# Threshold attention and a squared-relu MLP on one core: the sign of the weight rounding moves to ScalarE, and the first steps are started differently

## The chip, the cores and the metric

The kernel runs on one core of one Trainium2 chip. The metric is the device time of one execution in microseconds; before the change it is 1410.58 us (median of three runs, 1410.53 to 1411.54). The profile comes from one execution of the same program, which took 1409.49 us; its recorded instructions span 1407.7 us. The engines are named as the profile names them: PE is TensorE, PEld its weight loads, DVE is VectorE, ACT is ScalarE, POOL is GpSimd, SP is SyncE. A name with a q (SPq) is the engine's queue, where it issues transfers.

## The reference

An attention over 8 batches of 8 heads, 576 positions and 64 values a head, in which a score counts only if it lies within tau of its row's maximum; then a two-layer MLP on the 4608 rows of 512 values.

```python
scores = scale * np.matmul(q, k.transpose(0, 1, 3, 2))          # scale 1/8
thresh = np.max(scores, axis=-1, keepdims=True) - tau
scores = np.where(scores >= thresh, scores, -1000000000.0)
scores = scores - np.max(scores, axis=-1, keepdims=True)
attn = np.exp(scores)
attn = attn / (np.sum(attn, axis=-1, keepdims=True) + 1e-09)
x = np.matmul(attn, v)                                          # heads side by side: 4608 x 512
h = x @ w_in                                                    # w_in 512 x 2048
r = np.maximum(h, 0.0)
out = (r * r) @ w_out                                           # w_out 2048 x 512
```

The weights come in as 64-bit words of double-precision numbers, seen as pairs of 32-bit halves, and the kernel rounds them to fp32 itself.

## The kernel before, in words

**Visits and steps.** Two heads of a batch make a pair, and pairs are taken in visits. A visit's step handles 128 query rows of both heads; the 64 rows that are left over get a step of their own. For the first batch each pair is visited twice: the first two row blocks of all four pairs, then their rest, so that the first 256 tokens of the MLP are complete early. `steps` lists (visit, row block); the first two steps belong to visit 0, the third to visit 1.

**One step.** `scores(s)` multiplies q and k into two PSUM tiles of two banks each, `s0` and `s1` (L251), one for each head, and VectorE takes each row's maximum (L273). `exponents` lets ScalarE compute the bias and the threshold (L281, L282) and the exponential (L284). `threshold` compares the scores with the threshold, multiplies and sums (L296), and takes a reciprocal (L298, L299). `divide` scales on GpSimd (L304, L306). Two steps later `turn` transposes the result on TensorE against the identity into banks 4 to 7 (L330), ScalarE copies it to `wT` (L331), and `mix` multiplies with v (L432). The tiles `s0` and `s1` have one buffer each: L296 is their last reader, so the next step's scores wait for it. q and k are brought into matmul layout on VectorE (L230, `prep`); at a visit's last step the q and k of the next visit are prepared between `exponents` and `threshold`.

**The MLP** works in chunks of 256 tokens. `fill` takes its pieces from a queue and puts them between the attention's stages by a planner that spreads them over the remaining steps; L480 is the first layer, L490 and L491 relu and square, L516 the second layer of the first chunk, L549 that of the others, done with seven products in place of eight from sums of weights (L504) and of activations.

**Rounding the weights.** 32 pieces of 128 x 512 words are loaded into three areas in turn (`load_weights`, L125) and rounded in five stages (`round_weights`), spread over steps before the first MLP pieces need them. `words` is the raw data; `hi` and `lo` are every second 32-bit word of it. Stage 0, on ScalarE: `e` is the high half, read as an fp32 number and scaled by 2 to the -112 (L137), and `d` the low half, scaled (L138). Stage 1, on VectorE: the sign bit of `hi` is masked out (L140); `e` shifted left by 3 is combined with it (L141), which gives the upper part `t`. Stage 2: sign and exponent of `t` are masked out (L144). Stages 3 and 4, on GpSimd: `d` times that (L146), and added to `t` into the weights' place (L148). In most steps stage 1 stands on VectorE between the maxima and the thresholds; at a visit's last step, and for the second piece of a step that has two, it stands behind the thresholds.

**Order.** All five engines are scheduled by hand: each runs its instructions in the order in which the program lists them. Loads of q, k and v are issued by SyncE (`load_qk`, L173 and L175, `load_v`, L213), for the first visit by SyncE and ScalarE in turn, and later by GpSimd (L194). The two k loads of L175 in a visit are small: the last 64 rows of the odd head. The program has eight semaphores for the transfers of these two hardware queues, which are taken in turn. The identity, tau (L57, L58) and some constants (L79, L240) are set up at the head of the program.

Of the kernel before, what the change touches and what calls it, by code (L numbers as in the profile page):

```python
# [19 lines left out]
def kernel(  # L20
# [31 lines left out]
    psum = ctx.enter_context(tc.tile_pool(name="psum", bufs=1, space=bass.MemoryType.PSUM))  # L52

    ident = const.tile([P, P], FP32, name="ident")
    make_identity(nc, ident)
    ntau8 = const.tile([P, 1], FP32, name="ntau8")
    nc.gpsimd.dma_start(out=ntau8, in_=tau.to_broadcast([P, 1]))  # L57
    nc.vector.tensor_scalar(out=ntau8, in0=ntau8, scalar1=-1.0 / SCALE, scalar2=None, op0=ALU.mult)  # L58

    w_in_sb = const.tile([P, NMC, d_ff], FP32, name="w_in_sb")  # L60

# [14 lines left out]

    vs = [const.tile([P, 2 * NBLK + 2, D], FP32, name=f"vs{i}") for i in range(2)]
    qmid = const.tile([P, P], FP32, name="qmid")
    nc.gpsimd.memset(qmid, 0.0)  # L79
    at = RAW * 2 * WP  # L80
    w_slots = [const.tile([P, 2, S], FP32, name=f"w{i}") for i in range(2)]
    w_slots.append(spare[:, at:at + 2 * S].rearrange("p (u k) -> p u k", u=2))
# [16 lines left out]
    p5s = const.tile([P, HD], FP32, name="p5s")  # L99
    u_sum = const.tile([P, HD], FP32, name="u_sum")  # L100
    osb = const.tile([P, 2, d_model], FP32, name="osb")
    bank = {i: psum.tile([P, 512], FP32, tag=f"bank{i}", name=f"bank{i}") for i in range(4, 8)}


    n_in = d_ff // WP * NMC
# [14 lines left out]
    def weight_area(i):  # L120
        at = (i % RAW) * 2 * WP
        return spare[:, at:at + 2 * WP]
# [4 lines left out]
    def round_weights(i, stage):  # L127

        words = weight_area(i).bitcast(U32).rearrange("p (n w) -> p n w", w=2)
        lo, hi = words[:, :, 0], words[:, :, 1]
        t, e, d = (turned[:, (i % 3 * 3 + x) * WP:(i % 3 * 3 + x + 1) * WP] for x in range(3))
        tu, eu = t.bitcast(U32), e.bitcast(U32)
        if stage == 0:
            nc.scalar.activation(out=e, in_=hi.bitcast(FP32), func=AF.Copy, scale=2.0 ** -112)  # L137
            nc.scalar.activation(out=d, in_=lo, func=AF.Copy, scale=2.0 ** -52)  # L138
        elif stage == 1:
            nc.vector.tensor_scalar(out=tu, in0=hi, scalar1=0x80000000, scalar2=None, op0=ALU.bitwise_and)  # L140
            nc.vector.scalar_tensor_tensor(out=tu, in0=eu, scalar=3, in1=tu, op0=ALU.logical_shift_left,  # L141
                                           op1=ALU.bitwise_or)
        elif stage == 2:
            nc.vector.tensor_scalar(out=eu, in0=tu, scalar1=0xFF800000, scalar2=None, op0=ALU.bitwise_and)  # L144
        elif stage == 3:
            nc.gpsimd.tensor_tensor(out=d, in0=d, in1=e, op=ALU.mult)  # L146
        else:
            nc.gpsimd.tensor_tensor(out=weight_piece(i)[1], in0=t.rearrange("p (h d) -> p h d", h=2),  # L148
                                    in1=d.rearrange("p (h d) -> p h d", h=2), op=ALU.add)
# [11 lines left out]
    def load_qk(n):  # L161


        if by_dma(n):
            load_part(k, n)
            load_part(q, n)
            return
        for x, t in ((rows_of(n)[1], k), (rows_of(n)[0], q)):
            for m in range(4):
                src, to = rows_32(t, n, m), x[m * 32:(m + 1) * 32, :, :]  # L170
                queue = nc.scalar if n == 0 and m % 2 else nc.sync
                last = REST // 32 if t is k and m >= 2 else 0
                queue.dma_start(out=to[:, last:, :], in_=src[:, 0:S // 32 - last, :])  # L173
                if last:
                    queue.dma_start(out=to[:, 0:last, :], in_=src[:, S // 32 - last:, :])  # L175

    def load_part(t, n):
# [58 lines left out]
    LITTLE = 2.0 ** -20  # L236

    stats = [const.tile([P, 8, 2], FP32, name=f"st{i}") for i in range(4)]
    for st in stats:
        nc.gpsimd.memset(st[:, 4, :], S * LITTLE)  # L240
    weights = {}

    def scores(s):


        vis, i = steps[s]
        n = 2 if i < NBLK or paired(vis) else 1
        sc = [psum.tile([P, 2, 512], FP32, tag=f"s{u}", name=f"s{u}") for u in range(n)]

        def term(u, half, rows, lhsT, keys, to=slice(0, P)):  # L250
            nc.tensor.matmul(sc[u][to, half, 0:HALF], lhsT, keys[rows, half * HALF:(half + 1) * HALF],  # L251
                             start=True, stop=True)

        if i == NBLK and paired(vis):
            for half in range(2):
                for v_ in range(2):
                    for u in range(2):
                        rows, cols = slice(u * D, (u + 1) * D), slice(v_ * D, (v_ + 1) * D)
                        term(u, half, rows, qmid[rows, cols], kT[v_], cols)
        elif i == NBLK:  # L260
            for half in range(2):
                term(0, half, slice(0, P), qmid, kT[vis % 2])
        else:
            halves = [(half, u) for half in range(2) for u in range(n)]
            if early():
                halves.sort(key=lambda x: x[1])
            for half, u in halves:
                rows = slice(u * D, (u + 1) * D)
                term(u, half, rows, qT[rows, i * P:(i + 1) * P], kT[vis % 2])
        st = stats[s % len(stats)]  # L270
        mx = st[:, 0, 0:n]
        for u in range(n):
            nc.vector.tensor_reduce(out=mx[:, u:u + 1], in_=sc[u][:, :, 0:HALF], axis=AX.XY, op=ALU.max)  # L273

        w = w_slots[(s - first_dma) % (2 if by_dma(vis) else 3)][:, 0:n, :]
        weights[vis, i] = w, sc, st

    def exponents(vis, i):
        w, sc, st = weights[vis, i]
# [457 lines left out]
            prep_at[d].append(lambda n=nxt: prep_part(k, n + 1))  # L737

    load_qk(0)
    load_qk(1)  # L740
    load_v(0)
    for i in range(RAW):
        load_weights(i)
    prep(0)
    done = 0
    rounded_by = [0]
    for s in range(END + 1):
        state["step"] = s
        state["usable"] = rounded_by[-1]
        rounded_by.append(state["rounded"])  # L750
        on = s < NST
        now = []
        if on:
            n, i = steps[s]
            at = visits[n][1].index(i)
            last = at == len(visits[n][1]) - 1
            now = list(range(done, done + pieces[s]))
            done += pieces[s]
            more = n + 1 < len(visits)
            short = n < 2 * HP  # L760
            if short and at == 0 and 0 < n + 1 < 2 * HP:
                load_qk(n + 2)
            elif not short and at == 1 and not by_dma(n):
                load_qk(n + 1)
            if now:
                round_weights(now[0], 0)
            scores(s)
        old = steps[s - 2] if 2 <= s < NST + 2 and not by_dma(steps[s - 2][0]) else None
        at_once = now or old or early()
        lay = on and last and more and not by_dma(n)  # L770
        if old:
            turn(*old, 0)
            turn(*old, 1)
        if on:
            exponents(n, i)
            for p in now[1:]:
                round_weights(p, 0)
            if at == 1:
                split_left(n)
            if lay:  # L780
                prep(n + 1)
            elif now:
                round_weights(now[0], 1)
        if s in mixes and not old:
            mix(*mixes[s])
            for j in chunk_at.get(s, ()):
                add_chunk(j)
        quarter = rate(s) / 4 if s < END else 1e9
        fill(quarter)
        if s in mixes and old:  # L790
            mix(*mixes[s])
            for j in chunk_at.get(s, ()):
                add_chunk(j)
        if old:
            turn(*old, 2)
        state["free"] = s > first_dma
        if on:
            threshold(n, i)
            for fn in prep_at[s] + load_at[s]:
                fn()  # L800
            if lay and now:
                round_weights(now[0], 1)
            if now:
                round_weights(now[0], 2)
                round_weights(now[0], 3)
            for p in now[1:]:
                for stage in range(1, 4):
                    round_weights(p, stage)
            if not at_once:
                divide(n, i)  # L810
        if 0 < s <= NST and by_dma(steps[s - 1][0]):
            m, x = steps[s - 1]
            turn_blocks(m, x)
        for what in place_at[s]:
            place_blocks(*what)
        some_loads()
        fill(quarter)
        some_loads()
        if on and at_once:
            divide(n, i)  # L820
        fill(quarter)
        some_loads()
        fill(quarter)
        some_loads()
        if on:
            for p in now:
                end_rounding(p)
            if at == 0 and 0 < n <= 2 * HP:
                load_v(n)
            elif last and n >= 2 * HP and not by_dma(n):  # L830
                load_v(n + 1)
# [35 lines left out]
```

## Time and profile before

| what | us |
|---|---|
| time, median of three | 1410.58 |
| span of the profile | 1407.7 |
| MLP first layer, L480, TensorE busy | 522.3 |
| scores, L251, TensorE busy | 175.7 |
| rounding on VectorE, L140, L141, L144, busy | 18.0, 30.3, 17.6 |
| rounding on ScalarE, L137, L138, busy | 21.9, 21.5 |
| rounding on GpSimd, L146 and twice L148, busy | 41.0, 21.3, 21.3 |
| first rounding instruction starts | 19.5 |
| last one ends | 233.0 |

A busy time is a sum over all instructions of a row. Engines work beside each other, so such sums are not parts of the span: what an edit is worth depends on what else waits at that place. The column "idle before" of a row says how long its engine stood still ahead of those instructions, and "<-" what released it. The clock column gives the share of full speed that TensorE was granted by the records; before the first recorded change, at about 28 us, it shows 1.00 whatever the clock was.

### The profile page before, as it was taken

The page shows a single profiled execution, that of the slowest core. Times are in us where ns is not written, and L with a number is a line of the kernel's source. Part 1 is how long each engine was busy: PE and PEld are TensorE (multiplying, and loading weights), DVE is VectorE, ACT ScalarE, POOL GpSimd, SP SyncE. Part 2 cuts the span into 40 slices and gives each one's busy share as a digit, 9 for nine tenths or more (in the row PEclk, how much of TensorE's full clock was granted, in tenths as well). Part 3 has the DMA queues.
Part 4 walks back from the last instruction along what each step waited for, and adds up shares of the span by engine and source line. Part 5 has one row for each costly group of instructions (what it writes and reads, how often), then busy time and mean ns, then how long its engine had stood idle before and what let it go on. Part 6 is the DMA issues. An engine that isn't in the chain of part 4 may idle for free.

```text
span 1407.7 us, 22706 instructions
## 1 busy us (share of the span) xinstructions
PE 1359.6 (97%) x7556; PEld 1041.7 (74%) x7556; DVE 855.8 (61%) x1898; ACT 440.0 (31%) x1068; POOL 917.3 (65%) x1231
## 2 busy tenths in 40 slices
PE   5898998999999999999999999999999999999998
PEld 3676655767777777777777877777777877788887
DVE  5888785886767676766575666666666666501001
ACT  3775664323232323222222222222222222210110
POOL 3688778667787767777777858585867665422332
PEclk9998999999999999999999999999999999999999
DMA  7664441236555555554535455544545544310000
GB/s 150 135 143 124 117 104 42 59 71 122 107 115 98 118 99 111 101 104 85 107 82 111 99 111 96 101 82 102 93 98 95 123 83 97 64 38 15 1 16 16
DMA packets 397989, 127.95 MB, mean 91 GB/s; under 512 B 380464, under 2 KB 386672, under 8 KB 397872
## 3 DMA queue, kind: packets, MB, share of 16 engines
q1 hardware_dynamic: 374576, 93.07, 35.0%
q0 software_dynamic: 20912, 33.13, 8.6%
q8 instruction: 61, 1.00, 0.3%
q10 hardware_dynamic: 2384, 0.30, 0.1%
q14 instruction: 56, 0.46, 0.1%
HBM read 50.59 MB, written 9.44 MB: 43 GB/s over the span
## 4 chain that ended last, share of the span: by engine, by line
PE 88%; DVE 5%; ACT 2%; issue 2%; POOL 2%; DMA 1%; POOLq 0%; DVEq 0%; ACTq 0%
PE bank L480 34%; PE bank L549 28%; PE s L251 12%; PE bank L432 10%; PE bank L516 2%; PE bank L330 1%; DVE st L273 1%; DVE w L296 1%; DVE wo L504 1%; ACT w L284 1%; ACT wT L331 1%; DVE turned L141 1%; POOL kl L194 0%; DMA ql<-in_q_dram 0%; POOL w L306 0%
## 5 line engine op out<-in xcount | busy, mean ns | idle before, releaser
L480 PE MATMUL bank<-xT,w_in_sb 128*128 128x256 f32 x2304 | 522.3, 384 | 1.1 <-ACT osb L522 1.1
L480 PEld LDWEIGHTS bank<-xT,w_in_sb 128*128 128x128 f32 x2304 | 433.2, 191 | 83.3 <-issue 22.2
L273 DVE TENSOR_REDUCE st<-s 128x1 f32<-128x576 f32 x288 | 205.9, 752 | 231.2 <-PE s L251 231.1
L296 DVE SCALAR_TENSOR_TENSOR w<-s,st,w 128x576 f32<-128x576 f32 x269 | 209.2, 815 | 110.1 <-ACT w L284 109.9
L549 PE MATMUL bank<-wo,gsum 128*128 128x256 f32 x1088 | 248.9, 382 | 2.2 <-POOL gsum L470 2.1
L306 POOL TENSOR_SCALAR w<-w,st 128x576 f32<-128x576 f32 x269 | 223.3, 838 | 25.5 <-DVE st L299 19.3
L549 PEld LDWEIGHTS bank<-wo,gsum 128*128 128x128 f32 x1088 | 203.9, 190 | 41.3 <-issue 9.8
L491 POOL TENSOR_TENSOR g<-g 128x512 f32<-128x512 f32 x144 | 151.7, 1054 | 97.1 <-ACT g L490 95.6
L281 ACT ACTIVATE st<-st 128x2 f32<-128x2 f32 (+1 forms) x148 | 30.3, 205 | 576.5 <-DVE st L273 576.0
L251 PE MATMUL s<-kT,qT 64*128 64x288 f32 x1024 | 175.7, 440 | 32.2 <-DVE w L296 13.9
L549 PE MATMUL bank<-wo,g 128*128 128x256 f32 x816 | 188.3, 382 | 0.0
L284 ACT ACTIVATE w<-s,st 128x576 f32<-128x576 f32 x269 | 183.1, 731 | 0.2 <-ACT st L282 0.2
L304 POOL TENSOR_SCALAR st<-st 128x2 f32<-128x2 f32 (+1 forms) x148 | 34.2, 231 | 223.7 <-DVE w L296 213.8
L370 DVE STREAM_TRANSPOSE turned<-w 128x512 f32<-128x512 f32 (+2 forms) x388 | 168.8, 489 | 16.2 <-DMA wT<-turned 14.0
L549 PEld LDWEIGHTS bank<-wo,g 128*128 128x128 f32 x816 | 153.0, 190 | 30.0 <-issue 8.7
L432 PE MATMUL bank<-wT,vs 128*64 128x128 f32 (+7 forms) x1700 | 167.9, 356 | 4.1 <-ACT wT L331 3.7
L251 PEld LDWEIGHTS s<-kT,qT 64*128 64x128 f32 x1024 | 99.5, 191 | 91.9 <-issue 64.4
L432 PEld LDWEIGHTS bank<-wT,vs 128*64 128x64 f32 (+1 forms) x1700 | 95.7, 136 | 77.5 <-issue 23.5
L490 ACT ACTIVATE g<-bank 128x512 f32<-128x512 f32 x144 | 86.1, 599 | 197.0 <-PE bank L480 196.3
L194 POOL DMA_DIRECT2D vs<-in_v_dram x144 | 90.7, 634 | 0.0
L563 DVE TENSOR_TENSOR gsum<-g 128x512 f32<-128x512 f32 x34 | 22.8, 701 | 110.6 <-PE bank L549 110.6
L194 POOL DMA_DIRECT2D kl<-in_k_dram x100 | 68.9, 692 | 0.0
(73 smaller groups left out, 1015.1 us busy)
## 6 DMA issues: line engine op xcount, KB each, us to landing
wT<-turned SPq DMA_DIRECT2D x800, 72.0 KB, 2.3
out_dram<-osb POOLq DMA_DIRECT2D x34, 256.0 KB, 2.7
wo<-in_moe_w_in_dram SPq DMA_DIRECT2D x16, 512.0 KB, 4.7
wo<-in_moe_w_out_dram SPq DMA_DIRECT2D x16, 512.0 KB, 3.7
kl<-in_k_dram POOLq DMA_DIRECT2D x100, 72.0 KB, 3.0
ql<-in_q_dram POOLq DMA_DIRECT2D x100, 72.0 KB, 2.7
wT<-turned SPq DMA_DIRECT2D x192, 36.0 KB, 2.2
vs<-in_v_dram POOLq DMA_DIRECT2D x50, 128.0 KB, 3.1
```

The source lines that it names most:

```text
L194: nc.gpsimd.dma_start(out=to, in_=src)
L251: nc.tensor.matmul(sc[u][to, half, 0:HALF], lhsT, keys[rows, half * HALF:(half + 1) * HALF], start=True, stop=True)
L273: nc.vector.tensor_reduce(out=mx[:, u:u + 1], in_=sc[u][:, :, 0:HALF], axis=AX.XY, op=ALU.max)
L284: nc.scalar.activation(out=w[:, u, :].rearrange("p (h k) -> p h k", h=2), in_=sc[u][:, :, 0:HALF], func=AF.Exp, bias=bias[:, u:u + 1], sca ...
L296: nc.vector.scalar_tensor_tensor(out=wu, in0=sc[u][:, :, 0:HALF], scalar=thr[:, u:u + 1], in1=wu, op0=ALU.is_ge, op1=ALU.mult, accum_out=s ...
L306: nc.gpsimd.tensor_scalar(out=w[:, u, :], in0=w[:, u, :], scalar1=z[:, u:u + 1], scalar2=rcp[:, u:u + 1], op0=ALU.add, op1=ALU.mult)
L370: nc.vector.transpose(wb[:, at:at + k1 - k0, i % 2, :], w[:, u, k0 * 32:k1 * 32].rearrange("p (k q) -> p k q", q=32))
L432: nc.tensor.matmul(ps[u * D:(u + 1) * D, :], vs[n % 2][rows, u * (NBLK + 1) + c, :], wT[rows, NBLK if c == NBLK else u * (NBLK + 1) + c, a ...
L480: nc.tensor.matmul(h[:, x % 2, :], w_in_sb[:, c, f * P:(f + 1) * P], xT[:, c, at:at + TCH], start=(c == 0), stop=(c == NMC - 1))
L490: nc.scalar.activation(out=to, in_=h, func=AF.Relu)
L491: nc.gpsimd.tensor_tensor(out=to, in0=to, in1=to, op=ALU.mult)
L549: nc.tensor.matmul(to, left[:, f, :], wo[:, slot, f, :], start=(f == 0), stop=(f == HF - 1))
```

## The change

It has three parts.

The rounding's sign: `e` is now made by a parametric relu with slope -2 to the 32 for negative inputs, where it was a copy. A negative input so becomes a positive number with an exponent higher by 32, and the shift left by 3 turns that into the sign bit. VectorE only shifts, and masks in stage 2 as before. VectorE reads no raw word any more.

The start: the small k loads of the first visit are issued by GpSimd, in the first place; identity, tau and constants are set up after them; the tau scaling on VectorE moves behind the first q and k transposes; and 20 transposes of the identity run on TensorE ahead of the first scores.

The second step's scores go into four PSUM banks of their own, `second`, are issued right behind the first ones, and their maxima are taken ahead of the first thresholds. From the third step on these banks are banks 4 to 7.

```diff
+    startup = ExitStack()
+    spsum = startup.enter_context(tc.tile_pool(name="spsum", bufs=1, space=bass.MemoryType.PSUM))
+    second = [spsum.tile([P, 2, 512], FP32, name=f"second{u}") for u in range(2)]
+    bank = {}
...
         if stage == 0:
-            nc.scalar.activation(out=e, in_=hi.bitcast(FP32), func=AF.Copy, scale=2.0 ** -112)
+            nc.scalar.activation(out=e, in_=hi.bitcast(FP32), func=AF.Prelu, scale=2.0 ** -112, alpha=-2.0 ** 32)
             nc.scalar.activation(out=d, in_=lo, func=AF.Copy, scale=2.0 ** -52)
         elif stage == 1:
-            nc.vector.tensor_scalar(out=tu, in0=hi, scalar1=0x80000000, scalar2=None, op0=ALU.bitwise_and)
-            nc.vector.scalar_tensor_tensor(out=tu, in0=eu, scalar=3, in1=tu, op0=ALU.logical_shift_left,
-                                           op1=ALU.bitwise_or)
+            nc.vector.tensor_scalar(out=tu, in0=eu, scalar1=3, scalar2=None, op0=ALU.logical_shift_left)
...
                 if last:
+                    queue = nc.gpsimd if n == 0 else nc.sync
                     queue.dma_start(out=to[:, 0:last, :], in_=src[:, S // 32 - last:, :])
...
-        sc = [psum.tile([P, 2, 512], FP32, tag=f"s{u}", name=f"s{u}") for u in range(n)]
+        sc = [second[u] if s == 1 else psum.tile([P, 2, 512], FP32, tag=f"s{u}", name=f"s{u}")
+              for u in range(n)]
...
+    def keep_busy(times):
+
+        for x in range(times):
+            nc.tensor.transpose(second[1][:, 1, x % 4 * P:x % 4 * P + P], ident, ident)
...
     load_qk(0)
+    make_identity(nc, ident)
+    nc.gpsimd.dma_start(out=ntau8, in_=tau.to_broadcast([P, 1]))
+    nc.gpsimd.memset(qmid, 0.0)
+    for st in stats:
+        nc.gpsimd.memset(st[:, 4, :], S * LITTLE)
     load_qk(1)
...
     prep(0)
+    nc.vector.tensor_scalar(out=ntau8, in0=ntau8, scalar1=-1.0 / SCALE, scalar2=None, op0=ALU.mult)
+    keep_busy(20)
...
         state["step"] = s
...
+        if s == 2:
+            startup.close()
+            bpsum = ctx.enter_context(tc.tile_pool(name="bpsum", bufs=1, space=bass.MemoryType.PSUM))
+            bank.update((x, bpsum.tile([P, 512], FP32, tag=f"bank{x}", name=f"bank{x}")) for x in range(4, 8))
...
-            scores(s)
+            if s != 1:
+                scores(s)
...
         state["free"] = s > first_dma
+        if s == 0:
+            scores(1)
         if on:
             threshold(n, i)
```

More of the change, by code (lines that the diff above doesn't have):

```diff
@@ L54 @@
     ident = const.tile([P, P], FP32, name="ident")
-    make_identity(nc, ident)
     ntau8 = const.tile([P, 1], FP32, name="ntau8")
-    nc.gpsimd.dma_start(out=ntau8, in_=tau.to_broadcast([P, 1]))
-    nc.vector.tensor_scalar(out=ntau8, in0=ntau8, scalar1=-1.0 / SCALE, scalar2=None, op0=ALU.mult)
     w_in_sb = const.tile([P, NMC, d_ff], FP32, name="w_in_sb")
@@ L78 @@
     qmid = const.tile([P, P], FP32, name="qmid")
-    nc.gpsimd.memset(qmid, 0.0)
     at = RAW * 2 * WP
@@ L101 @@
     osb = const.tile([P, 2, d_model], FP32, name="osb")
-    bank = {i: psum.tile([P, 512], FP32, tag=f"bank{i}", name=f"bank{i}") for i in range(4, 8)}
+    startup = ExitStack()
+    spsum = startup.enter_context(tc.tile_pool(name="spsum", bufs=1, space=bass.MemoryType.PSUM))
+    second = [spsum.tile([P, 2, 512], FP32, name=f"second{u}") for u in range(2)]
+    bank = {}
     n_in = d_ff // WP * NMC
@@ L238 @@
     stats = [const.tile([P, 8, 2], FP32, name=f"st{i}") for i in range(4)]
-    for st in stats:
-        nc.gpsimd.memset(st[:, 4, :], S * LITTLE)
     weights = {}
```

## The prediction

> **What bounds the kernel now.** I read the page first: engine shares, then the slices.
>
> ```profile
> PE 1359.6 (97%) x7556; PEld 1041.7 (74%) x7556; DVE 855.8 (61%) x1898; ACT 440.0 (31%) x1068; POOL 917.3 (65%) x1231
> ...
> PE   5898998999999999999999999999999999999998
> ...
> PEclk9998999999999999999999999999999999999999
> ```
>
> TensorE is busy for 97% of the span and its slices (35 us each) fall under 9 only in the first seven. From about 300 us on it never stops, and its order of matmuls is the same in both programs. So the change can only win what TensorE idles, or runs at a low clock, before 300 us: 1407.7 - 1359.6 = 48 us of idle in all. Next, busy time by stretch of 20 us (columns: length, busy us of TensorE, its weight loads, VectorE, ScalarE, GpSimd, then clock, DMA share, GB/s):
>
> ```profile
> 0.00:20.00 20.00, 5.29 (x16) 3.10 (x16) 8.45 (x18) 4.95 (x10) 3.62 (x15) 1.00 0.68 147
> 20.00:40.00 20.00, 17.41 (x98) 12.66 (x99) 15.40 (x38) 10.93 (x27) 8.08 (x12) 0.91 0.74 136
> ...
> 100.00:120.00 20.00, 15.08 (x104) 11.61 (x103) 18.11 (x36) 13.43 (x35) 15.94 (x16) 0.85 0.43 126
> 120.00:140.00 20.00, 17.88 (x135) 13.45 (x134) 15.56 (x32) 12.23 (x30) 16.70 (x17) 0.93 0.40 121
> 140.00:160.00 20.00, 19.52 (x137) 14.21 (x135) 13.14 (x29) 12.83 (x33) 15.23 (x17) 0.88 0.39 97
> ```
>
> Idle is 14.7 us in the first 20 us, 2.6 in the next, 4.9 in 100 to 120, 2.1 in 120 to 140. Finer stretches show the clock at 0.50 from about 28.4 to 32, 114.3 to 121.4 and 137.8 to 144.3; the last two follow TensorE gaps of 3.8 us (at 111) and 1.9 us (at 135.4) and cost about 7/2 = 3.5 us each. The chain of waits names the start (start, us, what):
>
> ```profile
> 0.74 3.07 DMA kl<-in_k_dram
> 3.81 0.02 issue
> 3.83 3.01 DMA ql<-in_q_dram
> ...
> 8.36 2.30 PE s L251 x8
> ...
> 14.16 2.27 PE s L251 x6
> ...
> 20.15 2.99 PE s L251 x8
> ```
>
> The last q load is issued only when the first k load has landed. After that the first steps are a round trip of 6 us: scores, maximum on VectorE, exponents on ScalarE, threshold (L296), and only then the next scores, because they go into the same PSUM. The rounding's rows (busy us, mean ns | idle before):
>
> ```profile
> L141 DVE SCALAR_TENSOR_TENSOR turned<-turned 128x512 uint32<-128x512 uint32 x32 | 30.3, 947 | 2.9
> L137 ACT ACTIVATE turned<-wo 128x512 f32<-128x512 f32 x32 | 21.9, 686 | 0.2
> L140 DVE TENSOR_SCALAR turned<-wo 128x512 uint32<-128x512 uint32 x32 | 18.0, 563 | 0.0
> L144 DVE TENSOR_SCALAR turned<-turned 128x512 uint32<-128x512 uint32 x32 | 17.6, 550 | 0.3
> ```
>
> L140 lasts 0.415 at least and 1.35 at most, L141 0.691 and 1.65. The timeline shows where the long ones lie:
>
> ```profile
> 108.89 0.42 DVE L140 TENSOR_SCALAR turned<-wo 128x512 uint32<-128x512 uint32 x1
> ...
> 109.12 1.32 POOL L146 TENSOR_TENSOR turned<-turned 128x512 f32<-128x512 f32 x1 [1.15 <-ACT wT L331]
> 109.41 1.57 DVE L141 SCALAR_TENSOR_TENSOR turned<-turned 128x512 uint32<-128x512 uint32 x1
> ```
>
> GpSimd was inside L146; L141 ended 0.54 after it.
>
> **What the Trainium skill says.** "SBUF — State Buffer", Who interferes with whom: VectorE and GpSimd share a port pair as an exclusive lock, taken by a VectorE op in a 2-port mode or with two SBUF inputs; the later one blocks. The three lines above agree. "VectorE: DVE Perf Modes", the tier table: an fp32 tensor_scalar within SBUF runs at twice the rate of an op with two tensors; 0.42 against 0.69 agrees. So the new shift is short, but can still be blocked. "ScalarE: Activation LUTs", What ACT_TABLE_LOAD costs: one element per cycle whatever the function, about 93 ns more for an operand read by pointer. The trace has L281 at 205 and L282, with a pointer bias, at 281: 76 ns. "TensorE: Matmul & The Clock Gate", Part 1: the clock is halved or doubled by activity in windows of about 3.4 us; the first scores take 2.3 us to their first maximum, those at 33.2 us 1.24, which agrees. Its Part 4 says that transposes do not raise the clock; here scores and nine transposes from 20.15 to 25.25 were followed by fast scores at 27.05 (maximum after 1.29), which does not settle it.
>
> **The change, part by part.**
>
> 1. *First loads.* Two small k loads go from SyncE and ScalarE to GpSimd. The remaining eight on the two hardware queues no longer wait for a load to land (the program's waits show this). The last q issue moves from 3.83 to about 2.3, so it lands 3.0 later at 5.3; q transpose 0.71, k 0.73: scores could start at about 6.8. GpSimd's two issues cost 0.7 each (L57 took 0.70), end at 2.1 and land by about 5.
> 2. *Twenty transposes of the identity ahead of the scores.* The identity now follows those issues: 2.1 + 0.57 = 2.7. A cold transpose takes 2.18/9 = 0.242, so 20 take 4.85 and end at 7.6. They are queued in front of the scores, which therefore start at 7.6, not 6.8: against 8.36 a gain of **0.8**. If the clock rises half-way it is up to 1.5.
> 3. *Second scores into unused banks.* They follow the first at once. Cold: first maxima 9.9 to 11.35, second scores ready at 11.85, maxima to 13.3; meanwhile the exponents are done at 12.4; thresholds 13.3 to 14.95, sums 15.3, transposes of the next q and k (which stood behind the second maxima before, and now behind the first thresholds) to 16.75; scores of step 2 at 16.8 against 20.15. That is 3.35, of which 0.8 is part 2. In the warm case 15.4, so 4.75. Before, step 2's second half waited for a threshold (2.99 instead of 2.3), which held back transposes and the copies that ScalarE does ahead of the exponents: another 0.6. New wait: the transposes at step 2 take over the borrowed banks, so need the second thresholds (end about 18.4); scores of step 2 hold TensorE until 19.1, so it costs nothing. Parts 1 to 3: **-4.0**, ends -2.5 and -6.
> 4. *Prelu for Copy.* Same size, one table load in both programs. 0 to 32 x 0.093 = 3 us of ScalarE, which is 31% busy; I take 0.
> 5. *Rounding on VectorE.* Two ops, 48.3 us, become one shift of 0.42 (free, as L140 at best) to 0.56 (as L140 on average): 32 times that is 13.4 to 18.0, so VectorE loses 30 to 35 us of work. Most was free: in a usual step L140 and L141 (1.11) stand between the maxima and the thresholds, which wait about 1.0 for the exponents anyway. It counts where rounding stands behind the thresholds or is blocked. Step by step: around 70, the shift is blocked until 71.6 by L148 and ends 0.25 earlier; 105.6 to 111.4, two pieces with four blocked ops become shift and mask each, about 1.0 earlier; 129 to 134, the same, 1.0; 203 to 206, 0.4 (TensorE waited 0.37); 214 to 231, where GpSimd's own queue of divisions and loads is the chain, 0.4. Sum **-3.0**, ends 0 and -7.
> 6. *Clock.* If the gaps at 111 and 135.4 shrink by about 1 us each, a window may stay busy enough. Two drops at 3.5 us; I expect about 0.7 of a drop saved: **-2.5**, ends +3.5 (one more) and -7.
>
> Moved memsets and the tau load run while the first loads land. Sum: -4.0 - 3.0 - 2.5 = -9.5: 1410.6 - 9.5 = **1401**.
>
> **Rivals.**
> - *Only the start arrives:* shifts are blocked as L141 was, GpSimd (80% busy from 60 to 140) sets the pace, the clock drops as before: 1410.6 - 4.0 = 1406.6. For it: blocked ops end with GpSimd's op, whatever their own length. Against: four blocked ops in a pair of pieces become fewer.
> - *The middle opens up:* both drops vanish (-7), rounding at its end (-6), warm start (-5.5): 1392. For it: VectorE is 18.1 of 20 us busy in the gap at 111. Against: ScalarE and GpSimd follow closely.
> - *The start is eaten by the clock:* -4 and one more drop of 3.5: 1410.
> - *Slower:* GpSimd and VectorE trade the lock worse (0.15 a piece, 4.8), one more drop (3.5), with the start's 4: 1415. For it: the shift also locks out GpSimd's writes and descriptors. Against: VectorE holds the pair for less time in total.
>
> **How the numbers follow.** Forecast 0.55, only the start 0.24, middle opens 0.11, eaten 0.06, slower 0.04. Within 0.2% is 1407.8 to 1413.4, so faster 0.90, same 0.06, slower 0.04. The range 1394 to 1407.5 takes in the first two whole and the third in part, leaving out under 2 in 10.
>
> **What would show it.** Scores of step 2 at 15.4 to 17 rather than 20.15; VectorE at 821 to 826 us busy; the L137 row unchanged at 686 ns; the TensorE gap at 111 (shifted by 4) shorter, and one of the two later clock drops gone. Wrong if first scores start after 8.4, if a bank wait appears at the first transposes, if Prelu takes far over 0.78, or if gaps of the old size stand before 140 us.

## The result and the profile after

The kernel after takes 1397.95 us (median, 1395.52 to 1399.04) where the kernel before takes 1411.03 on the same chip: 13.1 us less, a ratio of 0.9905 with an interval of 0.9888 to 0.9922. The forecast was 1401.0 within 1394 to 1407.5. The profile of after comes from an execution of 1396.9 us, 12.6 less than the profiled one of before.

The page of after, engine shares and slices:

```profile
PE 1356.8 (97%) x7576; PEld 1042.1 (75%) x7576; DVE 830.8 (60%) x1866; ACT 439.5 (31%) x1068; POOL 909.7 (65%) x1233
...
PE   6898998999999999999999999999999999999998
...
PEclk8999999999999999999999999999999999999999
```

VectorE lost 25.0 us of work, ScalarE and GpSimd hardly changed. TensorE idles 1395.1 - 1356.8 = 38.3 us in all, where it was 48. From 300 us on its slices are full, as before. Some stretches of 20 us of after, with the columns of the prediction:

```profile
0.00:20.00 20.00, 11.21 (x45) 8.50 (x46) 9.34 (x22) 5.81 (x11) 5.31 (x19) 0.90 0.84 165
20.00:40.00 20.00, 17.56 (x117) 12.99 (x117) 15.26 (x34) 11.69 (x30) 9.74 (x14) 0.75 0.74 131
...
100.00:120.00 20.00, 17.08 (x130) 12.89 (x131) 15.13 (x30) 13.11 (x33) 17.97 (x21) 0.91 0.45 125
120.00:140.00 20.00, 19.21 (x153) 14.63 (x153) 15.39 (x31) 14.59 (x36) 17.18 (x19) 1.00 0.56 150
```

Of the 11.21 us in the first row 4.53 are the twenty transposes. From 100 to 140 TensorE idles 3.7 us and not 7.0, and the clock is 0.91 and 1.00 there, where it was 0.85 and 0.93. From 20 to 40 the clock reads 0.75 where it read 0.91: it was at half speed from 16.2 to 29.8. That is not a worse clock than before's, whose reading is too high in this stretch: its nine transposes at 23.07 took 2.18 us, just as long as the nine at 19.91 in after.

To see where the time went, mark the starts of the same scores in both traces: step 17 (counted from 0), after which come the two gaps of the prediction; step 22, behind both; step 35, behind the last rounding; step 43, in the stretch that no longer changes. "Half speed" is the time at clock 0.50 between steps 17 and 22, from stretches of half a microsecond. Most of the experiments, which are described below, are in the same table. Each row is one execution: those of e3, e4 and e6 are the slowest of their runs, those of e2 and e8 the fastest.

| kernel | step 17 starts | 17 to 22 | half speed there | 22 to 35 | 35 to 43 |
|---|---|---|---|---|---|
| before | 106.22 | 43.40 | 13.6 | 81.65 | 77.65 |
| after | 103.04 | 36.36 | 3.4 | 79.30 | 77.65 |
| e1_round_only | 105.46 | 36.37 | 3.4 | 79.14 | 80.75 |
| e2_start_only | 102.61 | 39.44 | 3.4 | 82.27 | 79.27 |
| e3_no_busy | 103.47 | 37.63 | 6.8 | 79.24 | 82.16 |
| e4_no_second | 105.22 | 37.71 | 6.8 | 79.33 | 82.16 |
| e6_mask_kept | 104.03 | 43.46 | 13.6 | 81.82 | 77.66 |
| e7_shift_twice | 102.02 | 41.45 | 10.2 | 80.58 | 82.17 |
| e8_fill_after | 98.79 | 37.36 | 3.4 | 79.30 | 79.19 |
| e9_hold_loads | 103.21 | 35.22 | 0 | 79.26 | 82.46 |
| e11_fill_after2 | 101.00 | 35.96 | 0 | 82.63 | 77.74 |

The gain of 12.6 us is 3.2 up to step 17, 7.0 from 17 to 22 and 2.4 from 22 to 35. After that the columns of before and after are equal.

**The start.** The timeline of after, TensorE and VectorE:

```profile
3.23 4.53 PE L280 MATMUL second<-ident 128*128 128x128 f32 x20 [3.23 <-POOL ident masks.py:199]
...
7.00 0.78 DVE L230 STREAM_TRANSPOSE qT<-ql 128x576 f32<-128x576 f32 x1 [7.00 <-DMA ql<-in_q_dram]
...
8.49 2.30 PE L250 MATMUL s<-kT,qT 64*128 64x288 f32 x8 [0.73 <-DVE ntau L754]
10.57 2.29 PE L250 MATMUL second<-kT,qT 64*128 64x288 f32 x8
17.69 2.30 PE L250 MATMUL s<-kT,qT 64*128 64x288 f32 x8 [4.82 <-DVE kT L230]
```

The first scores start at 8.49, no earlier than before (8.36). They waited for q, which landed at 7.0, not for the transposes, which end at 7.76. The start's gain is made by the third row of scores: step 1 needs no wait any more, so step 2 starts at 17.69 where it was 20.15.

**The rounding.** The rows of after, busy us and mean ns:

```profile
L141 DVE TENSOR_SCALAR turned<-turned 128x512 uint32<-128x512 uint32 x32 | 20.4, 637 | 0.0
L143 DVE TENSOR_SCALAR turned<-turned 128x512 uint32<-128x512 uint32 x32 | 19.8, 618 | 0.3
L138 ACT ACTIVATE turned<-wo 128x512 f32<-128x512 f32 x32 | 21.9, 685 | 1.9 <-DMA wo<-in_moe_w_in_dram 1.8
```

The parametric relu takes 685 ns where the copy took 686. The shift takes 637 ns on average though its shortest takes 407, and the mask, the same instruction as before, went from 550 to 618: part of the blocking moved from the op that is gone to the one that stayed. One piece of the two-piece step, timeline of after:

```profile
102.44 0.95 DVE L141 TENSOR_SCALAR turned<-turned 128x512 uint32<-128x512 uint32 x1
...
103.06 1.45 POOL L147 TENSOR_TENSOR w_in_sb<-turned 128x512 f32<-128x512 f32 x1
...
103.42 1.38 DVE L143 TENSOR_SCALAR turned<-turned 128x512 uint32<-128x512 uint32 x1
```

GpSimd's L147 ends at 104.51, the mask at 104.80, so here it is the mask that was held up until GpSimd was through. Still, two pieces and the maxima behind them are through sooner: in e2, which has the new start and the old rounding, the six ops of this step begin at 101.99 and the maxima at 107.75; here they are four, from 102.44, and the maxima begin at 106.46, 1.7 us less.

### The profile page after: what moved, and what is told of

Read it like the earlier page. It is cut to its first block, busy times and chain, and to the rows that moved or that the text cites. A ratio compares the mean times of both kernels' runs of the same rounds, so it can differ in the third digit from the quotient of the medians.

```text
span 1395.1 us, 22691 instructions
## 1 busy us (share of the span) xinstructions
PE 1356.8 (97%) x7576; PEld 1042.1 (75%) x7576; DVE 830.8 (60%) x1866; ACT 439.5 (31%) x1068; POOL 909.7 (65%) x1233
## 4 chain that ended last, share of the span: by engine, by line
PE 89%; DVE 4%; ACT 2%; issue 2%; POOL 2%; DMA 1%; POOLq 0%; DVEq 0%; SPq 0%; ACTq 0%
PE bank L484 35%; PE bank L553 28%; PE s L250 12%; PE bank L436 10%; PE bank L520 2%; PE bank L334 2%; DVE wo L508 1%; DVE w L300 1%; ACT w L288 1%; DVE st L272 1%; ACT wT L335 1%; POOL kl L194 0%; POOL w L310 0%; DVE turned L374 0%; DVE wo L300 0%
## 5 line engine op out<-in xcount | busy, mean ns | idle before, releaser
L310 POOL TENSOR_SCALAR w<-w,st 128x576 f32<-128x576 f32 x269 | 220.5, 829 | 25.2 <-DVE st L303 19.3
L250 PE MATMUL s<-kT,qT 64*128 64x288 f32 x1016 | 168.2, 435 | 19.4 <-DVE w L300 6.9
L250 PEld LDWEIGHTS s<-kT,qT 64*128 64x128 f32 x1016 | 95.4, 189 | 76.6 <-issue 56.5
```

Source lines behind the costliest of these rows:

```text
L310: nc.gpsimd.tensor_scalar(out=w[:, u, :], in0=w[:, u, :], scalar1=z[:, u:u + 1], scalar2=rcp[:, u:u + 1], op0=ALU.add, op1=ALU.mult)
```

## The experiments

The theory: the two parts are separate and add up. The start gains by the second scores, the rounding by shorter waits of the scores on VectorE and by fewer clock drops. The rivals were that one part carries all, that the parametric relu costs something, and that the clock, not the waits, makes the difference.

**Each part alone.** e1_round_only is before with the new rounding; e2_start_only is after with the old rounding.

```diff
# e1: before
-            nc.scalar.activation(out=e, in_=hi.bitcast(FP32), func=AF.Copy, scale=2.0 ** -112)
+            nc.scalar.activation(out=e, in_=hi.bitcast(FP32), func=AF.Prelu, scale=2.0 ** -112, alpha=-2.0 ** 32)
-            nc.vector.tensor_scalar(out=tu, in0=hi, scalar1=0x80000000, scalar2=None, op0=ALU.bitwise_and)
-            nc.vector.scalar_tensor_tensor(out=tu, in0=eu, scalar=3, in1=tu, op0=ALU.logical_shift_left,
-                                           op1=ALU.bitwise_or)
+            nc.vector.tensor_scalar(out=tu, in0=eu, scalar1=3, scalar2=None, op0=ALU.logical_shift_left)
# e2: after, with the same lines the other way round
```

> The kernel before with the parametric relu and the shift alone; the start as it was. Theory A (the rounding's VectorE work is what held TensorE at 97, 111 and 135 us, and the clock drops follow those gaps): 9 to 11 us of the gain is here, 1400 to 1402. Theory B (the gain in the middle comes from the start's shift of all alignments, the rounding is hidden or re-blocked): 1407 or more. The profile is to show VectorE at about 830 us busy and the scores of step 2 at 20.1.

> The changed start alone, rounding as before (mask, shift and combine on VectorE, copy on ScalarE). Theory A: 2.4 us, the shift that the profiles show between 36 and 60 us, so 1408.5, with both later clock drops in place. Theory B: 8 us or more, 1403 or less. The prediction's own figure for the start was 4.0, 1407.

Measured: e1 1402.35 (1399.96 to 1404.81), ratio 0.9938 [0.9926, 0.9951], 8.3 us less than before; e2 1405.69 (1404.19 to 1407.15), 0.9964 [0.9952, 0.9977], 5.0 less. Together 13.3; the whole change is 13.1. By the medians they add up, and the rounding is the larger part: e1 comes near the 9 to 11 of its theory A and far from B, and e2 gains more than the 2.4 of A. The table says where: e1 gains 0.8 up to step 17, 7.0 to step 22 and 2.5 to step 35, and loses 3.1 after that; e2 gains 3.6 up to step 17 and 4.0 to step 22, and loses 0.6 and 1.6 after that. Place by place the two do not add up: both profiled executions have 10.2 us less at half speed between steps 17 and 22, which after can have only once.

What separates wait from clock is a comparison of the waits between steps 17 and 22 (us in total, times, longest). Before:

```profile
PE s L251 <- DVE w L296: 5.7, 2, 3.8
```

e2_start_only:

```profile
PE s L252 <- DVE w L302: 5.7, 2, 3.8
```

After:

```profile
PE s L250 <- DVE w L300: 2.9, 2, 2.3
```

Before and e2 have the same two waits, yet e2 needs 39.44 us for this stretch and before 43.40: the difference of 4.0 is 10.2 us less at half speed, and nothing of the rounding's work. It is not the start's doing either: e6 below has e2's start and e2's work on VectorE, and in its profiled execution the half-speed time is before's 13.6 and the stretch 43.46. From e2 to after the half-speed time is the same, 3.4 us, and the waits fall by 2.8: 39.44 to 36.36, so 3.1 us are the rounding's own. In the sum of 7.0 of these executions the clock has 4.0 and the waits 3.1.

**The parametric relu and the two ops on VectorE.** e6_mask_kept is after with mask and combination kept behind the parametric relu; the combination then sets the same sign bit again. e7_shift_twice is after with the shift done twice.

```diff
# e6: after
-            nc.vector.tensor_scalar(out=tu, in0=eu, scalar1=3, scalar2=None, op0=ALU.logical_shift_left)
+            nc.vector.tensor_scalar(out=tu, in0=hi, scalar1=0x80000000, scalar2=None, op0=ALU.bitwise_and)
+            nc.vector.scalar_tensor_tensor(out=tu, in0=eu, scalar=3, in1=tu, op0=ALU.logical_shift_left,
+                                           op1=ALU.bitwise_or)
# e7: after
             nc.vector.tensor_scalar(out=tu, in0=eu, scalar1=3, scalar2=None, op0=ALU.logical_shift_left)
+            nc.vector.tensor_scalar(out=tu, in0=eu, scalar1=3, scalar2=None, op0=ALU.logical_shift_left)
```

> The changed kernel with the parametric relu on ScalarE, but mask and combine on VectorE as before (the same values, since the sign bit is then set twice). If Prelu costs nothing and the two ops on VectorE are all of the rounding's gain: as the changed start alone, 1405.7. If Prelu itself costs: later than that by what it costs. If the gain came from ScalarE or the loads: near 1398.

> The changed kernel with the shift done twice on VectorE (the second writes the same again): 32 more ops of 0.42 us when free, 0.64 as the shift is now on average. If VectorE's time in the rounding is what counts, in proportion: 13.4 to 20.4 of the 28 to 30 us that were taken away come back, so 4 to 6 of the 8.3 us: 1402 to 1404. If it is the two-input form alone that hurt: 1398 to 1399.

Measured: e6 1405.04 (1404.13 to 1407.58), the same as e2 with its 1405.69 within the spread, so the parametric relu costs nothing that these runs can see, and the rounding's gain is VectorE's. e7 1401.70 (1401.19 to 1407.31), 3.8 more than after, with 849.7 us of VectorE in place of 830.8: of 18.9 us of added work a fifth reaches the time. That is just under the first expectation and well above the second, for which the form with two inputs alone would have to count. In its profiled execution the stretches from 17 to 22 and from 22 to 35 are 5.1 and 1.3 us longer than after's; of that about 2.4 are the clock, an estimate from 6.8 us more at half speed and the price of such time worked out below.

**The two parts of the start.** e3_no_busy leaves the twenty transposes out; e4_no_second puts step 1's scores back into the usual tiles and place.

```diff
# e3: after
-    keep_busy(20)
+    keep_busy(0)
# e4: after
-        sc = [second[u] if s == 1 else psum.tile([P, 2, 512], FP32, tag=f"s{u}", name=f"s{u}")
+        sc = [psum.tile([P, 2, 512], FP32, tag=f"s{u}", name=f"s{u}")
               for u in range(n)]
...
-            if s != 1:
-                scores(s)
+            scores(s)
...
-        if s == 0:
-            scores(1)
```

> The changed kernel without the 20 transposes ahead of the scores. Theory A, that they warm nothing and hold nothing up (the q transpose starts at 7.0 and they end at 7.75, before the first scores at 8.49; scores cold all the same): within 1 us of the changed kernel's 1398. Rival, that their activity is what raised the clock at 13 us or sets the phase: 1 to 3 us slower.

> The changed kernel with the second step's scores in the usual tiles and at the usual place, loads, transposes and rounding as changed. If the second scores in unused banks are the whole of the start's gain: the scores of step 2 back at about 20.2, 2.4 to 3.2 us slower than the changed kernel, 1400.5 to 1401. If the earlier loads bring part of it, about 1 us less than that.

Measured: e3 1401.69 (1399.01 to 1403.07), 3.7 more than after; e4 1403.43 (1400.13 to 1404.98), 5.5 more. Both are more than was expected of them, and more than the start itself accounts for: at step 17 e3 is 0.4 behind after and e4 2.2. (e4's first scores ran at full clock and took 1.25 us, after's took 2.30; beside e7, whose first scores took 1.25 too, e4 is 3.2 behind.) The rest is later, in stretches whose code is the same in all three. The timeline of e3 behind GpSimd's loads, from step 35:

```profile
220.34 2.29 PE L250 MATMUL s<-kT,qT 64*128 64x288 f32 x8 [2.59 <-DVE wo L300]
222.56 1.54 PE L334 MATMUL bank<-ident,w 128*128 128x128 f32 x6
```

The same in after:

```profile
218.70 1.24 PE L250 MATMUL s<-kT,qT 64*128 64x288 f32 x8 [2.65 <-DVE wo L300]
219.87 0.88 PE L334 MATMUL bank<-ident,w 128*128 128x128 f32 x6
```

Both waited 2.6 us for the same threshold. In e3 the clock is at half speed from 219.5, within that wait, for 6.8 us; in after it stays full. The last column of the table is made of this: 77.65 with no such time, 79.27 with 3.4 us of it (e2), 80.75 with 6.8 (e1), 82.16 with 10.2 (e3, e4): about 1.5 us for each 3.4. Between steps 17 and 22, with the new rounding, it is 35.22 (e9), 36.36 and 37.63 (e3; e4 has 37.71) for 0, 3.4 and 6.8: 1.2 each. Why the same wait halves the clock in one execution and not in the other can be read from the traces. Up to 340 us, the changes of the clock in all fourteen lie on grids of 3.41 us, whose position against the program differs between executions. The windows of these grids around the two waits, with the columns of the prediction; e3:

```profile
216.07:219.49 3.42, 1.68 (x23) 1.10 (x19) 1.45 (x3) 1.75 (x6) 3.21 (x5) 1.00 0.18 43
219.49:222.90 3.41, 2.56 (x10) 1.61 (x11) 1.29 (x5) 0.00 (x0) 3.22 (x5) 0.50 0.00 0
```

After:

```profile
214.15:217.56 3.41, 1.90 (x23) 1.31 (x23) 1.16 (x2) 1.97 (x6) 3.20 (x5) 1.00 0.17 43
217.56:220.97 3.41, 2.27 (x15) 1.68 (x16) 2.34 (x7) 0.52 (x2) 3.22 (x5) 1.00 0.00 0
```

In e3 most of the wait falls into one window, which is left 49% busy; in after it is shared between two, with 56% and 67%. Over all fourteen traces, the clock was halved behind all 35 full-speed windows in which TensorE was under 44.5% busy, behind 10 of the 35 between that and 62%, and behind none of the 1193 above. So a wait of 2.6 us can go either way. The transposes' 3.7 us by the medians is a lead of 0.4 in the first hundred microseconds and, in the profiled execution, clock drops that fell differently. Whether leaving the transposes out moves the grid to a worse place, or five runs happened to have more drops, was not settled.

**Holding the loads of visit 1.** They are issued from 3.78 on in after, from 5.42 on before, and q landed late; e9_hold_loads makes them wait for q.

```diff
# e9: after
+    nc.vector.tensor_copy(rows_of(1)[1][:, 0:1, 0:1], rows_of(0)[0][:, 0:1, 0:1])
     load_qk(1)
```

> The kernel after, but the loads of visit 1 (and what SyncE issues behind them) wait until the last q load of visit 0 has landed, by a copy of one column on VectorE. Theory: in the kernel after, q lands at 7.0 and not at the predicted 5.3 because these loads, issued from 3.78 on, share the transfer engines with it. Then q lands at about 5.3 to 5.8, and the first scores are set by the twenty transposes, 7.2 to 7.8 instead of 8.49; the visit-1 rows land at about 10 to 12, still ahead of their use at 16.1; the time falls by 0.5 to 1.2 us against after. Rival: q's landing is set by its own issue and the packets' own length; then it stays near 7.0, and the time within 1 us of after, or up to 3 us longer because the weights arrive later.

Measured: 1401.31 (1397.69 to 1403.46), 3.4 more than after. The timeline of VectorE in e9:

```profile
6.72 0.15 DVE L749 COPY wo<-ql 128x1 f32<-128x1 f32 x1 [6.72 <-DMA ql<-in_q_dram]
```

q lands 0.3 earlier, not 1.2 to 1.7: the theory of shared bandwidth holds for a small part only. With almost nothing else on the way, the transfer engines are busy from 2.0 to 5.6 us in e9 with the first visit's loads, eight of 64 or 72 KB, some 560 KB, at 127 to 183 GB/s. That this volume sets q's landing is likely; a run with fewer bytes was not made. And the held loads cost something on the other side. ScalarE's row in e9:

```profile
20.13 0.66 ACT L138 ACTIVATE turned<-wo 128x512 f32<-128x512 f32 x1 [5.94 <-DMA wo<-in_moe_w_in_dram]
```

The first weights are issued behind the held loads, at 15.61 in place of 12.59; the parametric relu waits for them, and the exponents of step 2 stand behind it on ScalarE. So step 2 starts at 15.82, 1.9 before after's, and step 3 at 24.02, 0.1 later than after's. In the profiled execution e9 is level with after at step 17 and its whole loss is clock: from 35 to 43 it takes 82.46, with 10.2 us at half speed, in place of 77.65. Whether the 3.4 us of the medians come from there was not shown.

**Filling the gaps with transposes.** If gaps lower the clock, work that nobody needs should keep it up. e5_fill_before puts transposes ahead of the scores of steps 18 and 21 in before, into a bank of 4 to 7; e10_spare_fill does the same into columns of the score banks that nothing reads. e8_fill_after is after with fills like e5's, at the start too (at step 2 into a score tile); e11_fill_after2 is after with fills like e10's; e12_all is e11 with e9's hold.

```diff
# e10: before; e11, e12: after, with FILL = {2: 20, 3: 8, 18: 14, 35: 15, 41: 15}
+    def spare_fill(s, times):
+
+        to = weights[steps[0 if s == 2 else s - 1]][1][0]
+        for x in range(times):
+            nc.tensor.transpose(to[:, x % 2, HALF:HALF + P], ident, ident)
...
+    FILL = {18: 20, 21: 10}
...
+            if s in FILL:
+                spare_fill(s, FILL[s])
             scores(s)
# e5: before, the same places and FILL, but written into a bank
...
+        to = bank[(4, 5)[(used["tx"] + 1) % 2]]
+        for x in range(times):
+            nc.tensor.transpose(to[:, x % 4 * P:x % 4 * P + P], ident, ident)
# e8: after, as e5, with a score tile at step 2
...
-    keep_busy(20)
+    keep_busy(23)
+    FILL = {2: 10, 3: 8, 18: 14, 21: 5, 35: 15}
```

> The kernel before, with 20 and 10 transposes of the identity on TensorE in its gaps at 111 and 135 us (ahead of the scores of steps 18 and 21, into a bank that is free then); nothing else moves. If the clock drops after these gaps cost what their length says (two times 6.9 us at half speed), 5 to 7 us faster, 1404 to 1405.5, with no drop at 113 and 137 us. If the drops are hidden behind VectorE and GpSimd, no change, 1410.

> The kernel before, with 20 transposes of the identity ahead of the scores of step 18 (gap of 3.8 us at 111) and 10 ahead of step 21 (gap of 1.9 us at 135.4), written into columns of the score banks that nothing reads, so that they need wait for no copy, which the earlier fill did. Theory (the gaps cost more through the clock than by themselves): the drops at 113.5 and 137.6, 6.8 us of half speed each, go, and the time falls by 5 to 7 us. Rival (most of the half-speed time falls on stretches where TensorE would wait anyway): scores start where they did, and the time falls by less than 2 us.

> The changed kernel with more transposes of the identity in TensorE's idle time: 23 at the start in place of 20, 10 ahead of the scores of step 2 (into their own tile, free by then), 8 ahead of step 3, and 14, 5 and 15 in the gaps at 107, 129 and 216 us. If the clock is the main part of what is left: no drop at 111 and 220, cold only before about 20 us, 3 to 6 us faster, 1392 to 1395, and a smaller spread between runs. If transposes do not hold the clock up: 1398, drops as before.

> The kernel after, with transposes of the identity into the same spare columns ahead of the scores of steps 2, 3, 18, 35 and 41 (20, 8, 14, 15, 15), where TensorE waits 4.8, 1.8, 2.3, 2.7 and 2.7 us. Theory: the half-speed stretches at 16.2 to 29.8 and 111.6 to 115 go, the first of which costs about 3 us of cold scores and transposes on the path and the second 1.7; 2 to 5 us faster than after. Rival: none of it is on the path, within 1 us of after.

> The kernel after with both: visit 1's loads held until q has landed, and the fills of the run before. If the two effects are real and separate, 3 to 6 us faster than after, that is 1392 to 1395; if either is not, no better than the better of the two runs before.

Measured: e5 1412.27 (1.0011 [1.0003, 1.0019]), e10 1412.81 (1.0016 [1.0010, 1.0023]), both a little slower than before; e8 1396.28 (1395.21 to 1401.34), e11 1399.11 (1397.36 to 1401.33), e12 1400.70 (1400.39 to 1401.27). None reached the gain that was hoped for. The timeline of e10 shows why its fills could not do their work:

```profile
115.74 4.53 PE L349 MATMUL s<-ident 128*128 128x128 f32 x20 [3.72 <-DVE w L296]
```

They did not run in the gap. They waited out the gap of 3.8 us themselves, for the last reader of the tile, although they write columns that it does not read, and then stood in front of the scores for 4.5 us. In e5 the fills waited in the same way, 3.65 us, for the copy to `xT`. So at steps 18 and 21 these runs do not test whether an unbroken TensorE keeps its clock. e11's fills at step 2 did better, since they wait only for an early threshold: they ran from 13.46 to 15.87, the scores of step 2 followed at 16.20 and took 1.25 in place of 2.30, and step 17 starts at 101.00, 2.0 ahead of after. At step 18 and above all at step 35, where the fills stood in front of the scores, that was given back: 22 to 35 takes 82.63.

Two of e8's fills did run inside their gaps. The timeline of e8, ahead of steps 3 and 35:

```profile
18.98 1.09 PE L353 MATMUL bank<-ident 128*128 128x128 f32 x8
...
212.72 1.86 PE L353 MATMUL bank<-ident 128*128 128x128 f32 x15
```

They waited for nothing, and step 35 follows step 34 in 6.62 us, as in after. Up to step 17 e8's profiled execution has 3.4 us at half speed on record in place of 13.6, and step 17 starts at 98.79: 4.2 ahead of after, and 3.2 ahead of e7, whose first scores were as fast as e8's (and which has some more work on VectorE). So work that nobody needs did keep the clock up in the first steps. A loss of 1.0 from 17 to 22 and a drop from 35 to 43 took part of the gain away. e8's median is 1.7 below after's, but the two overlap; no version was shown to beat after.

## Why the prediction was right, and where it was not

Faster, and inside the range, by a mechanism of the right kind; but the sum of -9.5 was -13.1, and several of its terms were mis-sized. In the profiled executions the start brought 2.4, the rounding 6.3 and the clock 4.0 us, where 4.0, 3.0 and 2.5 were forecast, so it was partly luck that the errors had different signs. Of its own marks two more were missed: VectorE is at 830.8 us and not at 821 to 826, and step 2 starts at 17.69 and not by 17.

1. *First loads: failed.* The step "lands 3.0 later at 5.3" took a time from issue to landing from before, where the last q load went out after others had landed. The q loads now take 3.9 and 4.3 us (median) and land at 7.0; e9 shows that the loads behind them add only 0.3 to that. The first scores start at 8.49, past the 8.4 that the prediction named as proof against itself, and this part gained nothing.
2. *Transposes: wrong limit.* 20 cold ones were right (4.53 against 4.85), but q, not they, set the start. Whether they raise the clock in time depends on the execution: in after and e6 the first scores took 2.30 us behind them, in e2, e4, e7, e8, e9, e11 and e12 1.25; without them, in before, e1, e3, e5 and e10, 2.30 each time. This answers the point that the prediction left open: the statement of the Trainium skill, "TensorE: Matmul & The Clock Gate", Part 4, that transposes do not engage the full clock, does not hold for these fp32 transposes, which were all that TensorE had done when the clock of e2 rose at 6.3 us, while its Part 1, a free-running window of about 3.4 us, fits both this and the half-speed stretches, which all last a multiple of 3.4.
3. *Second scores: right in kind, and the start as a whole too large.* Step 2 was forecast at 16.8 cold and 15.4 warm; it was 17.69 cold, which is the forecast plus the 0.9 by which the first scores were late, and 16.2 warm in e2. No bank wait appeared. e4 puts the part's size at 2.2 us at step 17, or at 3.2 beside e7. The start as a whole brings 3.6 at step 17 where the first scores ran at full clock (e2), but 2.2 where they ran at half (e6), and 2.4 in after if e1's 0.8 are taken from its 3.2. For the execution that was profiled the term of -4.0, and its near end of -2.5, were too large.
4. *Parametric relu: right*, by its row (685 ns) and by e6.
5. *Rounding: direction right, both sizes wrong.* VectorE's work fell by 25.7 us (65.9 to 40.2 in the rows), not by 30 to 35: the shift was priced free or as L140, and the mask at its old time, but on average both now take longer, where they meet GpSimd's ops. On the path it brought 6.3, not 3.0: 0.8 up to step 17 (e1), 3.1 from 17 to 22 (e2 to after), 2.4 from 22 to 35. The gap ahead of step 18 fell by 1.5, that ahead of step 21 by 1.35, each forecast at 1.0. The worst miss is at 203 to 206, forecast at the 0.37 that TensorE was seen to wait. Timeline of before:

```profile
206.64 1.70 PE L251 MATMUL s<-kT,qT 64*128 64x288 f32 x7 [0.37 <-DVE w L296]
207.97 0.40 PE L336 MATMUL bank<-ident,w 64*128 64x64 f32 x4
208.18 0.40 PE L251 MATMUL s<-kT,qT 64*128 64x288 f32 x1
```

The same scores in after:

```profile
194.71 1.24 PE L250 MATMUL s<-kT,qT 64*128 64x288 f32 x8
```

A group of scores whose second head must wait for its own threshold is booked as busy while it waits, 1.70 in place of 1.24, and its last matmul falls among the next transposes. From the end of the transposes ahead of them (206.27 and 194.78) to the next MLP piece (208.76 and 196.18) it is 2.5 us before and 1.4 after: 1.1, of which the wait view showed 0.37. Two more such rows, for which the prediction had no entry, start at 174.32 and 187.13 in before. The second, before:

```profile
187.13 1.95 PE L251 MATMUL s<-kT,qT 64*128 64x288 f32 x8
```

After:

```profile
176.25 1.33 PE L250 MATMUL s<-kT,qT 64*128 64x288 f32 x8
```

The steps with these two rows are 0.65 and 0.62 us shorter in after; with the 1.1 they make the 2.4 from 22 to 35. At 214 to 231, where 0.4 was forecast, step 34 to 35 takes 6.58 before and 6.62 after: nothing.

6. *Clock: near in the sum, by two errors.* A drop of 6.8 us was priced at 3.5, as if all of it were on TensorE's path; it costs about 2.4 to 3.0. And one and a half drops were saved between steps 17 and 22, not 0.7, which is 4.0 against 2.5 in the profiled execution. In the medians it is less: e1's 8.3 less the 6.3 of point 5 leaves 2.0. That shorter gaps cause fewer drops is plain at step 21 and less so at step 18. At step 21 the least busy window of 3.41 us was 45%, 45% and 51% with the old rounding (before, e6, e2), and the clock dropped in the first two; with the new one it was 71% to 84% in five profiles (after, e1, e3, e4, e9), without a drop. At step 18 it was 15% to 26% in the three, each with a drop, and 31% to 57% in the five, of which four had one. How many of the remaining drops a given run has is left to where its grid lies, so that the sum came near was in part luck.

The rival "only the start arrives" fails on e1. "The middle opens up" came nearer than its chance of 0.11 suggests: one of the two drops vanished and the other was halved, and the rounding came close to its end of -7. What held the time above 1392 were the start, with 2.4 in place of 5.5, and the clock, with 4.0 in place of 7.

## What to carry to other kernels

An op taken off VectorE here passed part of its blocked time on to the next op there: 48.3 us of ops became 20.4, and the mask behind them took 2.2 more. Count the gain from when the chain behind it gets through, not from the sum of the rows. Look for waits inside groups as well: a row of scores that lasts longer than its like is a wait that no wait view lists. And when versions differ by a few microseconds, cut the traces at common marks and compare stretch by stretch; here that told the waits that the edit took away from clock drops of 1.2 to 1.6 us for each 3.4, which otherwise look like effects of the edit.

## What the runs showed of the hardware that was not expected

- Twenty transposes of a 128 x 128 identity can raise TensorE's clock within themselves: 3.89 us for the twenty in e2 and the first scores at 1.25, against 4.53 and 2.30 in after, with the same start at 3.2.
- A gap of 2.6 us ahead of step 35 left the clock at full speed in after and halved it for 6.8 us in e3. The difference lies in how the gap fell on windows of 3.41 us: under 44.5% busy the clock was halved behind 35 of 35, over 62% behind none of 1193.
- Eight loads of 64 to 72 KB, issued between 0.7 and 2.9 us, kept the 16 transfer engines busy for 3.6 us in e9; the last of them was usable at 6.7 us there, and at 7.0 in after, where more loads followed at once.
